# A layer's products in pairs of 64 rows: 24 products of M2's first column group, in two PSUM banks

## The chip, the cores and the metric

The kernel runs on one core of one Trainium2 chip. The metric is the device time of one execution in microseconds (us). The median of three runs of the kernel before is 946.14 us (946.11 to 946.61).

## The reference

Attention with a sigmoid in place of the softmax feeds two layers of the same form (from a 768-wide token to 2048 and back). Only the last layer is touched by the change.

```python
scores = scale * np.matmul(q, k.transpose(0, 1, 3, 2)) - np.log(S)
attn = 1.0 / (1.0 + np.exp(-scores))
x = np.matmul(attn, v)            # 4 x 12 heads, 448 x 64, then tokens x 768
...
h = x @ w_in                      # layer 1: 1792 x 768 by 768 x 2048
g = s * np.maximum(h, 0.0) ** 2 + b
x = g @ w_out                     # 1792 x 2048 by 2048 x 768
...
h = x @ w_in                      # layer 2, the last one
g = np.maximum(h, 0.0) + alpha * np.minimum(h, 0.0)
out = g @ w_out
```

## The kernel before, in words

**Work.** After the attention stage each layer is done for two token groups of 2 x 512 and 2 x 384 tokens, one after the other, and for each group an "in" phase (`in_phase`, or `first_phase` for the very first) and an "out" phase (`out_phase`) follow. Each matrix product is taken by a seven-product scheme on 2 x 2 blocks (Strassen-Winograd): products M1 to M7 of sums and differences of the blocks, put together by additions. `out_phase` goes through them in the order M1, M2, M5, M6, M7, M4, M3 (`OUT_ORDER`, line 41), and for each through three column groups, k = 0, 1, 2, so it has 21 groups of products.

**A group of products.** The operands are full-precision numbers, each split into a rounded part ("hi", by a cast on ScalarE, line 519) and the rest ("lo", a subtraction on VectorE, line 522). For one piece of 128 rows of the contraction TensorE then does three products: hi weights by lo data, hi by hi, lo by hi. A group of `out_phase` has eight such pieces, 24 products of 128 rows, 128 output partitions and 512 or 384 columns, all added up in one PSUM bank. `mm_group` (lines 605 to 622) writes them; it is called once for each of three chunks of pieces (3, 3 and 2, `CHUNKS`).

```python
nc.tensor.matmul(d, wh_, ml_, start=first and k == 0, stop=False, **opt)
nc.tensor.matmul(d, wh_, mh_, start=False, stop=False, **opt)
nc.tensor.matmul(d, wl_, mh_, start=False, stop=last and k == n, **opt)
```

**Names.** `ring` holds the split weights of one group (three places, in turn, filled from `raw`, which SP's queue loads). `gb` holds the split data of a product, in three chunks: in the 512-column group gb_117 to gb_119 for M1 and gb_120 to gb_122 for M2. `g` holds the data before they are split; the differences that later products need are taken in place (line 532), and the layer's nonlinearity ends in a scale-and-add on VectorE (line 690). `tmp` holds what has been read out of PSUM.

**Banks.** There are eight. In `out_phase` M1's three column groups go to banks 0 to 2, those of M2 to banks 6, 7 and 6 (`6 + k % 2`), M5's to 3 to 5. When M2's group k has ended, VectorE adds the bank to `tmp` (`padd`, line 639), and the sum is stored.

**Order.** The program lists every operation with its engine, a duration and what it reads and writes (`Plan.add`). TensorE's order is the order of the list. For the other engines a planner (`Plan.order`, `Plan.place`) takes at each step the operation that can start first by its own estimates and, among those, the one that is needed soonest; a small random shift, drawn for each operation in the order of the list, is added to that due time. Each engine works through its order in sequence, and waits where an operand isn't ready or a buffer isn't free.

Of the kernel before, what the change touches and what calls it, by code (L numbers as in the profile page):

```python
# [17 lines left out]
P = 128  # L18
# [29 lines left out]
T = (512, 384)  # L48
# [25 lines left out]
class Plan:  # L74
# [9 lines left out]
    def add(self, eng, dur, fn, r=(), w=(), lat=0.06):  # L84
        i = len(self.ops)
        self.uses.append([sorted({c[1] for c in x if c[0] == "t"}) for x in (r, w)])
        r, w = ([c for c in x if c[0] != "t"] for x in (r, w))
        deps = set()
        for c in r:
            if c in self.writer:  # L90
                deps.add(self.writer[c])
        for c in w:
            if c in self.writer:
                deps.add(self.writer[c])
            deps.update(self.readers.get(c, ()))
        for c in r:
            self.readers.setdefault(c, set()).add(i)
        for c in w:
            self.writer[c] = i
            self.readers[c] = set()  # L100
        deps.discard(i)
        self.ops.append((eng, dur, lat, deps, fn))
# [149 lines left out]
def cells(r, n):  # L252
    a = r.base + r.off
    return [("t", r.of)] + [("s", c) for c in range(a // CELL, -(-(a + n) // CELL))]


def sb(r, n):
    return r.ap[:, r.off : r.off + n]
# [3 lines left out]
def tile_kernel(  # L262
# [11 lines left out]
    nc = tc.nc  # L274
# [3 lines left out]
    D = vt.shape[5]  # L278
# [21 lines left out]
    add = plan.add  # L300
# [64 lines left out]
    def dve_t(n, psum=False):  # L365
        return 0.075 + 1.037e-3 * n
# [8 lines left out]
    PE_LAT = 0.25  # L375
    MM = (0.2269, 0.1745)

    def tmp():
        return TMP.pop(0)

    def free(x):
        TMP.append(x)
# [102 lines left out]
    def unit(m, kind, i):  # L485
        at, n = i * UNIT, UNIT
        dst = entry(range(8 * i, 8 * i + 8))
        raw = RAW[n_unit[1] % NRAW]
        n_unit[1] += 1
        load(  # L490
            sb(raw, n), w32[m, kind][:, at : at + n], n,
            [("d", m, kind, 8 * i + j) for j in range(8)], cells(raw, n),
        )
        split(dst, dst + n, raw, n)
# [21 lines left out]
    def split(hi, lo, src, n, rows=1, step=None):  # L516
        (h, ch), (l, cl), (x, cx) = (part(r, n, rows, step) for r in (hi, lo, src))
        n *= rows
        add("ACT", act_t(n), lambda: nc.scalar.copy(h, x), cx, ch)  # L519
        add(  # L520
            "DVE", dve_t(n),
            lambda: nc.vector.tensor_tensor(  # L522
                out=l, in0=x, in1=h.bitcast(F32), op=ALU.subtract
            ),
            cx + ch, cl,
        )

    def minus(o, x, y, n, rows=1, step=None):
        (o_, co), (x_, cx), (y_, cy) = (part(r, n, rows, step) for r in (o, x, y))
        add(  # L530
            "DVE", dve_t(rows * n),
            lambda: nc.vector.tensor_tensor(out=o_, in0=x_, in1=y_, op=ALU.subtract),  # L532
            cx + cy, co,
        )
# [20 lines left out]
    def g_place(par, p, j=0):  # L555
        return G[par] + (8 * p + j) * T[par]
# [45 lines left out]
    def bank(k, n=S, c=0):  # L602
        return ps[:, k, c : c + n]

    def mm_group(par, dst_bank, terms, first, last, more=False):

        t = T[par]
        r = [("p", dst_bank)] if not first else []
        for wh, wl, mh, ml in terms:
            r += cells(wh, P) + cells(wl, P) + cells(mh, t) + cells(ml, t)  # L610

        def f():
            n = len(terms) - 1
            for k, (wh, wl, mh, ml) in enumerate(terms):
                wh_, wl_, mh_, ml_ = sb(wh, P), sb(wl, P), sb(mh, t), sb(ml, t)
                d = bank(dst_bank, t)
                opt = {"skip_group_check": more}
                nc.tensor.matmul(d, wh_, ml_, start=first and k == 0, stop=False, **opt)  # L618
                nc.tensor.matmul(d, wh_, mh_, start=False, stop=False, **opt)  # L619
                nc.tensor.matmul(d, wl_, mh_, start=False, stop=last and k == n, **opt)  # L620

        add("PE", 3 * MM[par] * len(terms), f, r, [("p", dst_bank)], PE_LAT)

    def pcopy(dst, k, n, func=None):
        d = sb(dst, n)

        def f():
            if func is None:
                nc.scalar.copy(d, bank(k, n))
            else:  # L630
                nc.scalar.activation(d, bank(k, n), func)

        add("ACT", act_t(n, True), f, [("p", k)], cells(dst, n))

    def padd(dst, k, other, n, c=0):
        d, o = sb(dst, n), sb(other, n)
        add(
            "DVE", dve_t(n, True),
            lambda: nc.vector.tensor_tensor(out=d, in0=bank(k, n, c), in1=o, op=ALU.add),  # L639
            [("p", k)] + cells(other, n), cells(dst, n),  # L640
        )
# [157 lines left out]
    def store(dst, src, n, w):  # L799
        d, x = dst, sb(src, n)  # L800
        add("SP", dma_t(n), lambda: nc.sync.dma_start(out=d, in_=x), cells(src, n), w, DMA_LAT)

    def put(m, g, p, k, src):

        row, nb = divmod(p, 2)
        dc = 2 * k + row
        t = T[g]
        if m == 0:
            kh, i = divmod(dc, KH)
            o = (2 * kh + nb) * XB[g] + i * t  # L810
            store(x_dram[1, g][:, o : o + t], src, t, [("x", 1, g, 2 * kh + nb, i)])
        else:
            c = 2 * g * T[0] + nb * t
            store(out[dc * P : (dc + 1) * P, c : c + t], src, t, [])

    def out_phase(m, g, par, middle):
        t, r = {}, {}
        P1, P2, P3, P4 = range(4)
        make = {
            "M1": (P1, None), "M5": (P1, (P2, P1)), "M2": (P3, None), "M6": (P1, (P4, P1)),  # L820
            "M7": (P2, (P4, P2)), "M4": (P1, (P3, P1)), "M3": (P4, None),
        }

        def prepare(i):
            src, diff = make[OUT_ORDER[i]]
            for (j0, j1), o in zip(CHUNKS, GB[par][i % 2]):
                n = (j1 - j0) * T[par]
                if diff:
                    minus(g_place(par, src, j0), g_place(par, diff[0], j0), g_place(par, diff[1], j0), n)
                split(o, o + n, g_place(par, src, j0), n)  # L830

        prepare(0)
        for i, x in enumerate(OUT_ORDER):
            if i + 1 < 7:
                prepare(i + 1)
            if i in middle:
                middle[i]()
            for k in range(NDP):
                unit(m, "out", i * NDP + k)
                bk = {"M2": 6 + k % 2, "M5": 3 + k, "M3": 3 + k}.get(x, k)  # L840
                more = x in ("M6", "M7", "M4", "M3")
                for (j0, j1), o in zip(CHUNKS, GB[par][i % 2]):
                    terms = [
                        (*ring[(i * NDP + k) * 8 + j], o + (j - j0) * T[par], o + (j1 - j0 + j - j0) * T[par])
                        for j in range(j0, j1)
                    ]
                    mm_group(par, bk, terms, not more and j0 == 0, j1 == 8, more)
                if x == "M1":
                    t[k] = tmp()
                    pcopy(t[k], bk, T[par])  # L850
                elif x == "M2":
                    padd(t[k], bk, t[k], T[par])
                    put(m, g, 0, k, t[k])
                    free(t[k])
                elif x == "M6":
                    r[k] = tmp()
                    pcopy(r[k], bk, T[par])
                elif x == "M7":
                    y = tmp()
                    pcopy(y, bk, T[par])  # L860
                    padd(y, 3 + k, y, T[par])
                    put(m, g, 3, k, y)
                    free(y)
                elif x == "M3":
                    padd(r[k], bk, r[k], T[par])
                    put(m, g, 1, k, r[k])
                    free(r[k])
                elif x == "M4":
                    y = tmp()
                    pcopy(y, bk, T[par])  # L870
                    put(m, g, 2, k, y)
                    free(y)
# [131 lines left out]
    for _ in range(NWARM):  # L1004
        for h in range(2):
            for j in range(2):
                rows = slice(j * D, (j + 1) * D)
# [3 lines left out]
                    start=True, stop=True,  # L1011
# [47 lines left out]
    for n, (m, g) in enumerate(phases):  # L1059
        par = n % 2  # L1060
# [79 lines left out]
```

## Time and profile before

| | |
|---|---|
| median of three runs | 946.14 us |
| the profiled execution | 946.52 us |
| its span, first to last instruction | 944.5 us |
| busy: TensorE products, VectorE, ScalarE | 938.5, 732.1, 650.7 us |
| the layers' products by 512 and by 384 columns, mean spacing in an undisturbed group | 0.227 and 0.173 us |
| M2 for k=0 in the last layer, 512-column group: start, start of the next group | 666.55, 671.99 us |
| the same, 384-column group | 865.07, 870.23 us |

A product's own duration in the trace (0.39 us at 512 columns) is longer than the spacing, since products are pipelined; what counts is from start to start. The same holds for VectorE: an operation of 1.75 us is followed by the next after 1.67 us.

### The profile page before, as it was taken

How to read it: one execution, taken by the hardware profiler on the slowest of the kernel's cores; microseconds unless marked ns; L12 is line 12 of the kernel's file. 1: busy time of each engine (PE TensorE's matmuls, PEld its weight loads, DVE VectorE, ACT ScalarE, POOL GpSimd, SP SyncE). 2: the span in 40 equal slices, each digit the busy share in tenths (PEclk: the TensorE clock that was granted, in tenths of full speed). 3: DMA queues.
4: the chain of work that ended last, by engine and by line, in shares of the span. 5: the costliest groups of instructions: out<-in, count | busy, mean ns of one | idle time of the engine just before them, and what ended most of it. 6: DMA issues, size and time to landing. Idle time of an engine off the chain costs nothing.

```text
span 944.5 us, 13900 instructions
## 1 busy us (share of the span) xinstructions
PE 938.5 (99%) x5424; PEld 778.5 (82%) x5424; DVE 732.1 (78%) x882; ACT 650.7 (69%) x796; POOL 0.2 (0%) x4
## 2 busy tenths in 40 slices
PE   9999999999999999999999999999999999999998
PEld 4333358888888889999999988888888899999998
DVE  1748668987999996677999959788985936689962
ACT  6989977868955754888967546667745536677551
POOL 0000000000000000000000000000000000000000
PEclk9999999999999999999999999999999999999999
DMA  8998999994647989898657787645334443443542
GB/s 303 324 317 304 335 312 316 322 303 158 239 145 243 316 297 339 306 311 271 227 165 238 229 291 236 234 132 193 120 113 122 149 141 112 134 135 120 151 136 96
DMA packets 81248, 210.88 MB, mean 223 GB/s; under 512 B 7712, under 2 KB 42912, under 8 KB 81184
## 3 DMA queue, kind: packets, MB, share of 16 engines
q1 hardware_dynamic: 81184, 210.01, 67.7%
q8 instruction: 42, 0.69, 0.3%
q14 instruction: 22, 0.18, 0.0%
HBM read 152.58 MB, written 57.41 MB: 222 GB/s over the span
## 4 chain that ended last, share of the span: by engine, by line
PE 88%; ACT 5%; DVE 5%; issue 2%; DMA 1%; DVEq 0%; ACTq 0%
PE ps L618 25%; PE ps L620 25%; PE ps L619 25%; PE ps L934 7%; PE ps L972 7%; DVE gb L522 1%; DVE ring L522 1%; ACT ring L519 1%; ACT g L706 1%; DVE g L639 1%; DMA raw<-w0in 1%; ACT neg L685 0%; ACT g L703 0%; ACT g L667 0%; ACT gb L519 0%
## 5 line engine op out<-in xcount | busy, mean ns | idle before, releaser
L618 PE MATMUL ps<-gb,ring 128*128 128x512 f32 (+1 forms) x672 | 243.4, 362 | 1.6 <-DVE gb L522 1.6
L619 PE MATMUL ps<-gb,ring 128*128 128x512 f32 (+1 forms) x672 | 243.0, 362 | 0.0
L620 PE MATMUL ps<-gb,ring 128*128 128x512 f32 (+1 forms) x672 | 243.0, 362 | 0.0
L519 ACT CAST ring<-raw 128x1024 fp32r<-128x1024 f32 x147 | 154.3, 1050 | 115.6 <-PE ps L619 102.3
L522 DVE TENSOR_TENSOR ring<-raw,ring 128x1024 fp32r<-128x1024 f32 x147 | 179.2, 1219 | 63.2 <-ACT ring L519 63.2
L620 PE MATMUL ps<-xo,ring 128*128 128x384 f32 (+1 forms) x504 | 177.6, 352 | 0.0
L619 PE MATMUL ps<-xo,ring 128*128 128x384 f32 (+1 forms) x504 | 177.6, 352 | 0.0
L618 PE MATMUL ps<-xo,ring 128*128 128x384 f32 (+1 forms) x504 | 177.6, 352 | 0.0
L618 PEld LDWEIGHTS ps<-gb,ring 128*128 128x128 f32 x672 | 126.1, 188 | 16.0 <-DVE gb L522 3.0
L620 PEld LDWEIGHTS ps<-gb,ring 128*128 128x128 f32 x672 | 126.1, 188 | 13.2
L619 PEld LDWEIGHTS ps<-gb,ring 128*128 128x128 f32 x672 | 126.1, 188 | 13.0
L522 DVE TENSOR_TENSOR gb<-g,gb 128x1536 fp32r<-128x1536 f32 (+3 forms) x84 | 116.3, 1395 | 13.1 <-ACT gb L519 7.1
L519 ACT CAST gb<-g 128x1536 fp32r<-128x1536 f32 (+3 forms) x84 | 99.3, 1196 | 23.0 <-PE ps L620 15.2
L619 PEld LDWEIGHTS ps<-xo,ring 128*128 128x128 f32 x504 | 94.6, 188 | 6.7
L620 PEld LDWEIGHTS ps<-xo,ring 128*128 128x128 f32 x504 | 94.6, 188 | 6.6
L618 PEld LDWEIGHTS ps<-xo,ring 128*128 128x128 f32 x504 | 94.6, 188 | 6.5
L950 ACT ACTIVATE sg<-ps,bias 128x896 f32<-128x896 f32 x84 | 83.4, 1013 | 13.5 <-PE ps L934 12.8
L639 DVE TENSOR_TENSOR g<-ps,g 128x512 f32<-128x512 f32 (+1 forms) x104 | 64.1, 623 | 23.8 <-PE ps L620 17.9
L934 PE MATMUL ps<-kq 64*64 64x448 f32 x672 | 78.5, 545 | 0.0
L972 PE MATMUL ps<-sg,v 64*64 64x448 f32 x672 | 77.1, 536 | 0.0
L532 DVE TENSOR_TENSOR g<-g 128x1536 f32<-128x1536 f32 (+3 forms) x48 | 66.0, 1391 | 0.0
L618 PE MATMUL ps<-xo,rinq 128*128 128x512 f32 x168 | 65.5, 390 | 0.0
(63 smaller groups left out, 993.8 us busy)
## 6 DMA issues: line engine op xcount, KB each, us to landing
r<-in_w_in SPq DMA_DIRECT2D x28, 768.0 KB, 6.3
raw<-w0out SPq DMA_DIRECT2D x42, 512.0 KB, 4.0
raw<-w1in SPq DMA_DIRECT2D x42, 512.0 KB, 3.6
raw<-w1out SPq DMA_DIRECT2D x42, 512.0 KB, 3.5
r<-in_w_out SPq DMA_DIRECT2D x18, 768.0 KB, 6.1
raw<-w0in SPq DMA_DIRECT2D x21, 512.0 KB, 5.4
kq<-in_qk SPq DMA_DIRECT2D x23, 448.0 KB, 4.8
w1out<-quada SPq DMA_DIRECT2D x6, 1344.0 KB, 7.5
```

What stands on the lines that cost most here:

```text
L519: add("ACT", act_t(n), lambda: nc.scalar.copy(h, x), cx, ch)
L522: lambda: nc.vector.tensor_tensor(out=l, in0=x, in1=h.bitcast(F32), op=ALU.subtract),
L532: lambda: nc.vector.tensor_tensor(out=o_, in0=x_, in1=y_, op=ALU.subtract),
L618: nc.tensor.matmul(d, wh_, ml_, start=first and k == 0, stop=False, **opt)
L619: nc.tensor.matmul(d, wh_, mh_, start=False, stop=False, **opt)
L620: nc.tensor.matmul(d, wl_, mh_, start=False, stop=last and k == n, **opt)
L639: lambda: nc.vector.tensor_tensor(out=d, in0=bank(k, n, c), in1=o, op=ALU.add),
L706: lambda: nc.scalar.activation(h, h, AF.Identity, bias=b_t, scale=s_t),
L934: nc.tensor.matmul(ps[h * D : (h + 1) * D, k + j, :S], a.ap[rows, S + k0 : S + k0 + D], a.ap[rows, :S], start=True, stop=True,)
L950: lambda: nc.scalar.activation(o, i, AF.Sigmoid, bias=sb(BIAS, 1), scale=QKSCALE),
L972: nc.tensor.matmul(ps[j * D : (j + 1) * D, k + h, :S], va[keys, v : v + D], a.ap[keys, j * S : (j + 1) * S], start=first, stop=last,)
```

## The change

In `out_phase` of the last layer, for M2 and k=0, every 128-row product becomes two 64-row products: rows 0 to 63 into bank 6 as before, rows 64 to 127 into bank 7. VectorE then adds both banks to `tmp`, one after the other. This is done once in each token group; nothing else in the code changes.

```diff
+                if other is not None:
+
+                    for i, (w, x) in enumerate(((wh_, ml_), (wh_, mh_), (wl_, mh_))):
+                        for b, rows in ((dst_bank, slice(0, D)), (other, slice(D, P))):
+                            nc.tensor.matmul(
+                                bank(b, t), w[rows], x[rows], start=first and k == 0 and i == 0,
+                                stop=last and k == n and i == 2, **opt,
+                            )
+                    continue
...
-        add("PE", 3 * MM[par] * len(terms), f, r, [("p", dst_bank)], PE_LAT)
+        w = [("p", k) for k in (dst_bank, other) if k is not None]
+        add("PE", 3 * MM[par] * len(terms), f, r + w[1:] if not first else r, w, PE_LAT)
...
-                    mm_group(par, bk, terms, not more and j0 == 0, j1 == 8, more)
+                    other = 7 if m == 1 and x == "M2" and k == 0 else None
+                    mm_group(par, bk, terms, not more and j0 == 0, j1 == 8, more, other)
...
                 elif x == "M2":
                     padd(t[k], bk, t[k], T[par])
+                    if other is not None:
+                        padd(t[k], other, t[k], T[par])
```

The planner keeps its old duration for the group. Since the list has one more operation in each of the two phases, the random shifts of all operations behind it are other ones, and the order moves a little around and after these places.

VectorE, 512-column group, around the addition of M2's group k=0 (tmp_90; ring_60 to ring_62 are the ring's places). Before:

```order
L522 TENSOR_TENSOR gb_117<-g_115,gb_117 128x1536
L522 TENSOR_TENSOR gb_122<-g_115,gb_122 128x1024
L532 TENSOR_TENSOR g_115<-g_115 128x1536
L522 TENSOR_TENSOR ring_62<-raw_68,ring_62 128x1024
L690 SCALAR_TENSOR_TENSOR g_115<-neg,nal,g_115 128x512
L522 TENSOR_TENSOR gb_118<-g_115,gb_118 128x1536
L639 TENSOR_TENSOR tmp_90<-ps,tmp_90 128x512
L690 SCALAR_TENSOR_TENSOR g_115<-neg,nal,g_115 128x512
```

The same place in the changed kernel:

```order
L522 TENSOR_TENSOR gb_122<-g_115,gb_122 128x1024
L522 TENSOR_TENSOR gb_117<-g_115,gb_117 128x1536
L532 TENSOR_TENSOR g_115<-g_115 128x1536
L522 TENSOR_TENSOR ring_62<-raw_68,ring_62 128x1024
L700 SCALAR_TENSOR_TENSOR g_115<-neg,nal,g_115 128x512
L522 TENSOR_TENSOR gb_118<-g_115,gb_118 128x1536
L700 SCALAR_TENSOR_TENSOR g_115<-neg,nal,g_115 128x512
L649 TENSOR_TENSOR tmp_90<-ps,tmp_90 128x512
L532 TENSOR_TENSOR g_115<-g_115 128x1024
L649 TENSOR_TENSOR tmp_90<-ps,tmp_90 128x512
L522 TENSOR_TENSOR ring_60<-raw_67,ring_60 128x1024
```

The split of gb_122 stands ahead of that of gb_117 now, one more scale-and-add stands ahead of the addition, and between the additions of the two banks there is a difference of 1024 columns.

TensorE, the end of M2's group k=0 and the start of group k=1 (on ring_61) in the changed kernel, with the engines that a product waits for:

```order
L622 MATMUL ps<-gb_122,ring_60 128x512 [waits DVE_49]
L622 MATMUL ps<-gb_122,ring_60 128x512
L622 MATMUL ps<-gb_122,ring_60 128x512 [waits Activation_49]
L622 MATMUL ps<-gb_122,ring_60 128x512 x9
L627 MATMUL ps<-gb_120,ring_61 128x512 [waits DVE_49]
```

Before, the last of these, the first product of k=1, had no wait; the products of the group k=0 were one row each and no pairs.

VectorE, 384-column group, from the addition of M2's group k=0 (tmp_86) on, in the changed kernel:

```order
L649 TENSOR_TENSOR tmp_86<-ps,tmp_86 128x384
L700 SCALAR_TENSOR_TENSOR g_116<-neg,nal,g_116 128x384
L649 TENSOR_TENSOR tmp_86<-ps,tmp_86 128x384
L522 TENSOR_TENSOR ring_60<-raw_67,ring_60 128x1024
L532 TENSOR_TENSOR g_116<-g_116 128x768
```

The third row is new; what stands before the first and the other rows are as before.

## Rows read from the trace of the kernel before

**Rows 1.** The page, part 1: TensorE's busy time.

```profile
PE 938.5 (99%) x5424; PEld 778.5 (82%) x5424; DVE 732.1 (78%) x882; ACT 650.7 (69%) x796; POOL 0.2 (0%) x4
```

**Rows 2.** Waits of TensorE, whole span, then from 672 us: total, times, longest.

```profile
PE ps L618 <- DVE gb L522: 1.6, 4, 0.7
...
PE ps L618 <- DVE gb L522: 1.2, 2, 0.7
```

**Rows 3.** Timeline of TensorE, 512-column group: start us, us, operation.

```profile
666.55 0.39 PE L618 MATMUL ps<-gb,ring 128*128 128x512 f32 x1
...
671.76 0.39 PE L620 MATMUL ps<-gb,ring 128*128 128x512 f32 x1
671.99 0.39 PE L618 MATMUL ps<-gb,ring 128*128 128x512 f32 x1
```

**Rows 4.** Timeline of TensorE, 384-column group.

```profile
865.07 0.33 PE L618 MATMUL ps<-gb,ring 128*128 128x384 f32 x1
...
869.08 0.44 PE L618 MATMUL ps<-gb,ring 128*128 128x384 f32 x1 [0.72 <-DVE gb L522]
869.36 0.34 PE L619 MATMUL ps<-gb,ring 128*128 128x384 f32 x1
...
870.06 0.33 PE L620 MATMUL ps<-gb,ring 128*128 128x384 f32 x1
870.23 0.33 PE L618 MATMUL ps<-gb,ring 128*128 128x384 f32 x1
```

**Rows 5.** Timeline of VectorE, 512-column group; [idle before <- what ended it].

```profile
664.87 2.89 DVE L522 TENSOR_TENSOR gb<-g,gb 128x1536 fp32r<-128x1536 f32 x2 [0.81 <-ACT gb L519]
667.68 1.75 DVE L532 TENSOR_TENSOR g<-g 128x1536 f32<-128x1536 f32 x1
669.35 1.22 DVE L522 TENSOR_TENSOR ring<-raw,ring 128x1024 fp32r<-128x1024 f32 x1
670.48 0.74 DVE L690 SCALAR_TENSOR_TENSOR g<-neg,nal,g 128x512 f32<-128x512 f32 x1
671.14 1.75 DVE L522 TENSOR_TENSOR gb<-g,gb 128x1536 fp32r<-128x1536 f32 x1
672.81 0.68 DVE L639 TENSOR_TENSOR tmp<-ps,tmp 128x512 f32<-128x512 f32 x1
673.41 0.74 DVE L690 SCALAR_TENSOR_TENSOR g<-neg,nal,g 128x512 f32<-128x512 f32 x1
```

**Rows 6.** Timeline of VectorE, 384-column group.

```profile
868.08 0.95 DVE L522 TENSOR_TENSOR gb<-g,gb 128x768 fp32r<-128x768 f32 x1
...
870.74 0.55 DVE L639 TENSOR_TENSOR tmp<-ps,tmp 128x384 f32<-128x384 f32 x1
871.21 0.61 DVE L690 SCALAR_TENSOR_TENSOR g<-neg,nal,g 128x384 f32<-128x384 f32 x1
871.74 1.21 DVE L522 TENSOR_TENSOR ring<-raw,ring 128x1024 fp32r<-128x1024 f32 x1
```

**Rows 7.** Chain that ended last, attention stage: start us, us, operation, records.

```profile
3.88 3.73 PE ps L934 x24
...
8.36 0.75 PE ps L934 x8
```

**Rows 8.** Timeline of TensorE, from the attention's last products to the first layer's.

```profile
129.21 2.42 PE L972 MATMUL ps<-sg,v 64*64 64x448 f32 x24
131.56 0.50 PE L618 MATMUL ps<-xo,rinq 128*128 128x512 f32 x1
```

**Rows 9.** DMA issues: KB each, median us to landing.

```profile
raw<-w1out SPq DMA_DIRECT2D x42, 512.0 KB, 3.5
```

**Rows 10.** Stretches: length, then busy PE, PEld, DVE, ACT, POOL, PEclk, DMA.

```profile
3.88:7.60 3.72, 3.72 (x28) 1.33 (x32) 0.00 (x0) 1.68 (x2) 0.00 (x0) 1.00 0.88 291
...
941.20:942.20 1.00, 0.00 (x0) 0.00 (x0) 0.51 (x1) 0.00 (x0) 0.00 (x0) 1.00 0.00 0
942.20:944.50 2.30, 0.00 (x0) 0.00 (x0) 0.00 (x0) 0.00 (x0) 0.00 (x0) 1.00 0.23 86
```

More of the change, by code (lines that the diff above doesn't have):

```diff
@@ L603, in bank, with mm_group @@
         return ps[:, k, c : c + n]
-    def mm_group(par, dst_bank, terms, first, last, more=False):
+    def mm_group(par, dst_bank, terms, first, last, more=False, other=None):
         t = T[par]
```

## The prediction

> **What bounds the kernel now.** I read the page's busy times first: TensorE is busy 938.5 us of a span of 944.5 us [rows 1], so the end moves only by what its stream gains or loses. The table of waits comes next: TensorE waits for splits on VectorE four times, 1.6 us in all, the longest 0.7 us [rows 2]. So a product slot saved is time saved, and a new wait of this engine is time lost, nearly one for one. After 672 us two waits are left, 1.2 us together [rows 2]; that is the most that a later stage could give back.
>
> Then the two places that the change touches. In the 512-column token group, M2 for k=0 starts at 666.55 us, its last product at 671.76 us, and the next group, M2 for k=1, at 671.99 us, with no gap [rows 3]: 5.44 us for 24 products, 0.227 us each. In the 384-column group it is 865.07 us to 870.23 us, with one wait inside, before the product at 869.08 us [rows 4]; the next group again follows without a gap. Last I read VectorE there. It adds the first bank at 672.81 us and 870.74 us [rows 5, 6], after the group has ended, and before the change nobody on TensorE waits for that.
>
> **Part 1: the products.** 24 products over 128 rows become 24 pairs over 64. No row shows a 64x128 pair; the nearest are the attention products, tiles of 64 rows by 64 columns in sets of four, of which two share the output partitions and go to two banks, as the new pairs do. Eight records (two sets) take 0.75 us [rows 7], so a set of 448 columns takes 0.375 us in two passes, 0.188 us a pass with four tiles side by side. Scaled by columns that is 0.188 x 512/448 = 0.215 us for a pair and 24 x 0.215 = 5.15 us for the group: 0.29 us less than 5.44. The other end is two halves one after the other: 48 x 0.227 = 10.9 us. I take the first, since the attention row is the same arrangement with more tiles. In the 384-column group the last six products wait for a split that VectorE ends at 868.08 + 0.95 = 869.03 us [rows 4, 6], so only six pairs can gain, under 0.1 us.
>
> TensorE changes from 128-row to 64-row tiles and back. The one change of that kind in the trace stands after the attention: the last 24 records (six sets of 0.375 us) start at 129.21 us, so the first full product was due at 131.46 us; it starts at 131.56 us [rows 8]. So 0.1 us each way at most, about what the pairs save in the first group. Neither counts if the next wait is longer, and it is.
>
> **Part 2: the wait.** This decides. Bank 7 now holds half of M2 for k=0, and M2 for k=1 writes into bank 7 next. Its first product must wait until VectorE has read the bank; before, that product had no wait (order on TensorE). Behind it stands the whole in-order stream of TensorE. VectorE also works in order, so the wait ends when it reaches the second addition.
>
> 512-column group. In the new order VectorE has, from the split of gb_117 on: split 1536, difference 1536, ring split, scale-and-add, split 1536, scale-and-add, addition of bank 6, difference 1024, addition of bank 7. The split of gb_117 started at 664.87 us, having waited 0.81 us for its cast [rows 5]. That cast sits behind the first pieces of M1's last group, which the change doesn't touch; the split of gb_122 now fills the wait ahead of it. So I start at 664.87 us and take the spacings of starts [rows 5]: 1536-column pass 669.35 - 667.68 = 1.67, ring or 1024-column pass 1.13, scale-and-add 0.66, addition 0.60. Sum 1.67 + 1.67 + 1.13 + 0.66 + 1.67 + 0.66 = 7.46, so bank 6 is added at 672.33 us; the group's last product ends by 671.76 + 0.39 = 672.15 us at the latest, so VectorE does not wait. Then 0.60 + 1.13 brings bank 7 to 674.06 us, and its 0.68 us to 674.74 us. From VectorE's end to TensorE's start it took 869.08 - 869.03 = 0.05 us [rows 4, 6]. So k=1 starts at 674.79 us instead of 671.99: **2.80 us**. Floor: additions back to back behind the last product, 672.15 + 0.60 + 0.68 + 0.05 = 673.48 us, 1.5 us. Ceiling: no idle time filled, and one scale-and-add (0.66) more ahead of 672.81 us: 673.47 + 0.60 + 1.13 + 0.68 + 0.05 = 675.93 us, 3.9 us.
>
> 384-column group. The order up to the addition of bank 6 is the old one, at 870.74 us [rows 6]; then a scale-and-add, then bank 7. So 870.74 + 0.47 + 0.53 = 871.74 us, + 0.55 + 0.05 = 872.34 us instead of 870.23: **2.11 us**. Floor, without the scale-and-add: 1.6 us; ceiling, with another scale-and-add slipping ahead: 2.6 us.
>
> Restart: after the wait at 869.08 us the second product came 0.28 us later instead of 0.173 [rows 4]; 0.1 us twice, **0.2 us**.
>
> **Costed at nothing.** The two additions themselves (0.60 and 0.47 us) lie behind the wait that is already counted; VectorE then is 0.6 us later but TensorE 2.8 us later, so it has more room than before for the splits of the next groups. The first store now waits for the second addition, and a load stands behind it on SP's queue; it is for M5's third group, which comes four groups of 5.44 us after k=1 starts, and a load lands in 3.5 us [rows 9]. In the 384-column group two loads move behind the stores of k=1 and k=2; they serve M6, three groups of 4.16 us after the later of these stores.
>
> **Sum**: 2.80 + 2.11 + 0.2 = 5.11 us. The profiled execution took 946.52 us, so it would take 951.6 us; the median of the three runs is 946.14 us, 0.38 us less, and I forecast against it: **951.3 us**, 0.54% slower. The floors give 949.4 us and the ceilings 952.8 us.
>
> **Rivals.**
> A. The pairs do not run side by side. For it: no row shows two tiles with 128 columns. Against it: the attention sets. If they run one after the other, the first group ends 5.44 us later, and VectorE's slack of 0.18 us (672.33 - 672.15) doesn't cover that: 5.3 us more. In the second, 48 products of 0.173 us from 865.07 us start the last one at 873.2 us, end it at 873.5 us, and 0.47 + 0.53 + 0.55 + 0.05 brings 875.1 us: 2.8 us more. Together 959.4 us. The Trainium skill ("TensorE: Matmul & The Clock Gate", Part 3, measured speedup) gives four row tiles only 3.07 times one. An estimate by that figure: a pair is 4/3.07 = 1.3 slots, the first group 7.1 us, and the time some 1.5 us above my forecast. The attention rows, where four tiles fit in 0.188 us a pass, speak against it; but those tiles are not row tiles alone.
>
> B. TensorE's clock falls in the wait. The wait of 3 us is four times the longest in the rows. At the start, with TensorE just out of idleness, 24 records took 3.73 us where 2.25 (three times 0.75) is usual [rows 7]: 1.5 us lost, although the granted clock reads 1.00, the higher of its two levels, there too [rows 10]. One fall gives 952.8 us, two 954.3 us. Against it: after the last product TensorE is idle from 941.2 us to the end at 944.5 us, and the granted clock still reads 1.00 [rows 10].
>
> C. Not slower: VectorE is ready in time. If it adds bank 7 so early that both waits together stay under 1.9 us, the result is no change, and if there is no wait at all, the pairs' 0.29 + 0.1 us give 945.8 us. For it: VectorE idles 0.81 us close before [rows 5]. Against: a floor of 1.5 + 1.6 us, as both additions can start only after the group's last product. It decides at a start of k=1 before 672.9 us and 871.2 us.
>
> **How the numbers follow.** A measurement of this kernel can tell about 0.2%, 1.9 us, from no change. My forecast, with the sizes between floors and ceilings: 0.78. A: 0.09. B: 0.10. C: 0.03. The range of 949.8 to 954.0 us reaches from near the floors (less part of the 1.2 us of later waits) through the ceilings to one fall of the clock and to pairs that overlap in part; it leaves out A's far end, C and two falls. Faster 0.01, same 0.03, slower 0.96.
>
> **What would show it.** In the table of waits, a new line of TensorE waiting for the addition into tmp on VectorE, twice, some 3 and 2 us. M2 k=0 in about 5.2 us, pairs starting 0.215 us apart; M2 k=1 starting near 674.8 and 872.3 us (the latter plus the first delay, 875.2 us). All groups after it at the old 5.44 and 4.16 us. Pairs 0.45 us apart would show A; products 0.45 us apart after the wait would show B; no wait and no shift would make the prediction wrong.

## The result, and the profile after

The changed kernel takes **954.79 us** (median of three runs, 954.52 to 955.07) against 946.14 us: a ratio of 1.009 (95% interval 1.0067 to 1.0113), slower as forecast, but by 8.65 us where 5.1 were forecast, and 0.8 us above the end of the range. The profiled execution took 954.79 us, with a span of 952.9 us against 944.5 us.

The waits of TensorE in the changed kernel (total, times, longest):

```profile
PE ps L627 <- DVE tmp L649: 4.6, 2, 2.7
...
PE ps L627 <- DVE gb L522: 0.6, 2, 0.5
PE ps L622 <- DVE gb L522: 0.5, 1, 0.5
```

The first line is new, and it is the one that the prediction named: TensorE waits twice for the addition into tmp. The waits for splits, 1.6 us before [rows 2], are 1.1 us now.

TensorE's timeline in the 512-column group, to be held beside [rows 3]:

```profile
666.10 0.39 PE L629 MATMUL ps<-gb,ring 128*128 128x512 f32 x1
666.42 5.76 PE L622 MATMUL ps<-gb,ring 64*128 64x512 f32 x48
674.85 0.50 PE L627 MATMUL ps<-gb,ring 128*128 128x512 f32 x1 [2.67 <-DVE tmp L649]
675.18 0.40 PE L628 MATMUL ps<-gb,ring 128*128 128x512 f32 x1
...
675.88 0.51 PE L628 MATMUL ps<-gb,ring 128*128 128x512 f32 x1
676.19 0.63 PE L629 MATMUL ps<-gb,ring 128*128 128x512 f32 x1
676.61 0.63 PE L627 MATMUL ps<-gb,ring 128*128 128x512 f32 x1
...
678.75 0.63 PE L629 MATMUL ps<-gb,ring 128*128 128x512 f32 x1
679.17 0.51 PE L627 MATMUL ps<-gb,ring 128*128 128x512 f32 x1
679.52 0.39 PE L628 MATMUL ps<-gb,ring 128*128 128x512 f32 x1
679.75 0.39 PE L629 MATMUL ps<-gb,ring 128*128 128x512 f32 x1
```

M2's second group starts at 674.85 us (forecast 674.79). Then comes what the sum did not hold: after five products at the usual pace, products start 0.43 us apart, at half pace, until 679.5 us. The stretches of the same time, and of the same thing in the 384-column group (columns as in [rows 10]; PEclk is the third number from the end), say why:

```profile
674.80:676.00 1.20, 1.15 (x5) 0.98 (x6) 1.20 (x2) 0.47 (x1) 0.00 (x0) 1.00 0.33 121
676.00:679.40 3.40, 3.40 (x10) 2.61 (x9) 3.40 (x3) 0.00 (x0) 0.00 (x0) 0.50 0.60 193
679.40:700.00 20.60, 20.60 (x92) 17.06 (x92) 16.11 (x14) 8.04 (x7) 0.00 (x0) 1.00 0.33 100
...
877.40:880.80 3.40, 3.40 (x12) 3.40 (x12) 3.40 (x4) 0.83 (x1) 0.00 (x0) 0.50 0.63 198
880.80:949.00 68.20, 68.20 (x394) 68.20 (x394) 39.86 (x39) 29.93 (x35) 0.00 (x0) 1.00 0.41 123
```

In two stretches the granted clock is 0.50, the lower of the two levels (1.2 instead of 2.4 GHz). Neither is a stretch of waiting: TensorE is busy throughout, and each begins after the products have come back, 1.2 us and 0.5 us after. The wait ahead of the second one, in the 384-column group, stands behind the shorter wait for a split that was there before [rows 4]:

```profile
873.68 1.32 PE L622 MATMUL ps<-gb,ring 64*128 64x384 f32 x12 [0.52 <-DVE gb L522]
876.94 0.44 PE L627 MATMUL ps<-gb,ring 128*128 128x384 f32 x1 [1.94 <-DVE tmp L649]
```

VectorE in the 512-column group, beside [rows 5]:

```profile
663.59 2.95 DVE L522 TENSOR_TENSOR gb<-g,gb 128x1024 fp32r<-128x1024 f32 x2
666.57 1.76 DVE L532 TENSOR_TENSOR g<-g 128x1536 f32<-128x1536 f32 x1
668.25 1.22 DVE L522 TENSOR_TENSOR ring<-raw,ring 128x1024 fp32r<-128x1024 f32 x1
669.38 0.74 DVE L700 SCALAR_TENSOR_TENSOR g<-neg,nal,g 128x512 f32<-128x512 f32 x1
670.04 1.75 DVE L522 TENSOR_TENSOR gb<-g,gb 128x1536 fp32r<-128x1536 f32 x1
671.71 0.74 DVE L700 SCALAR_TENSOR_TENSOR g<-neg,nal,g 128x512 f32<-128x512 f32 x1
672.38 0.68 DVE L649 TENSOR_TENSOR tmp<-ps,tmp 128x512 f32<-128x512 f32 x1
672.98 1.21 DVE L532 TENSOR_TENSOR g<-g 128x1024 f32<-128x1024 f32 x1
674.11 0.68 DVE L649 TENSOR_TENSOR tmp<-ps,tmp 128x512 f32<-128x512 f32 x1
```

The two additions start at 672.38 and 674.11 us; the prediction had worked out 672.33 and 674.06 us.

Where the time went, by groups of TensorE's products (from the first product of a group to the first of the next, us):

| group | before | after | more |
|---|---|---|---|
| 512 columns: M1 k=2, its end (change to 64-row tiles) | 5.44 | 5.53 | 0.09 |
| M2 k=0 with the wait behind it | 5.44 | 8.42 | 2.98 |
| M2 k=1 (start after the wait, slow stretch) | 5.44 | 7.17 | 1.73 |
| 384 columns: M1 k=2, its end | 4.16 | 4.25 | 0.09 |
| M2 k=0 with the wait behind it | 5.16 | 7.17 | 2.01 |
| M2 k=1 | 4.16 | 5.87 | 1.71 |
| sum | | | 8.61 |

All other groups of these phases are as before, and the sum is the difference of the spans (8.4 us) but for 0.2 us that this execution had gained earlier. So 5.2 us belong to waits and tile changes, and some 3.4 us to the two groups behind the waits (starts after a wait and slow stretches).

### The profile page after: what moved, and what is told of

Read it like the earlier page. It is cut to its first block, busy times and chain, and to the rows that moved or that the text cites. A ratio compares the mean times of both kernels' runs of the same rounds, so it can differ in the third digit from the quotient of the medians.

```text
span 952.9 us, 13996 instructions
## 1 busy us (share of the span) xinstructions
PE 942.8 (99%) x5472; PEld 781.2 (82%) x5472; DVE 734.3 (77%) x884; ACT 650.5 (68%) x796; POOL 0.2 (0%) x4
## 4 chain that ended last, share of the span: by engine, by line
PE 91%; DVE 5%; ACT 2%; issue 2%; DVEq 0%
PE ps L627 26%; PE ps L628 26%; PE ps L629 26%; PE ps L947 7%; PE ps L985 7%; DVE gb L522 2%; DVE ring L522 1%; DVE g L700 1%; DVE g L532 1%; ACT ring L519 1%; ACT neg L695 0%; DVE g L649 0%; ACT gb L519 0%; ACT g L697 0%; DVE tmp L649 0%
## 5 line engine op out<-in xcount | busy, mean ns | idle before, releaser
L627 PE MATMUL ps<-gb,ring 128*128 128x512 f32 (+1 forms) x656 | 239.0, 364 | 5.2 <-DVE tmp L649 4.6
L629 PE MATMUL ps<-gb,ring 128*128 128x512 f32 (+1 forms) x656 | 238.7, 364 | 0.0
L628 PE MATMUL ps<-gb,ring 128*128 128x512 f32 (+1 forms) x656 | 238.4, 363 | 0.0
L627 PEld LDWEIGHTS ps<-gb,ring 128*128 128x128 f32 x656 | 124.1, 189 | 19.9 <-DVE tmp L649 5.3
L628 PEld LDWEIGHTS ps<-gb,ring 128*128 128x128 f32 x656 | 124.1, 189 | 12.8
L629 PEld LDWEIGHTS ps<-gb,ring 128*128 128x128 f32 x656 | 123.9, 189 | 12.9
```

## The experiments

Theory 1: the waits for bank 7 cost what was worked out, and they also bring the two stretches at the lower clock. Its rivals: the 64-row pairs let the clock fall by themselves (theory 2), or the pairs are slow (theory 3). On the chip of the first four runs the kernel before took 946.81 us, on that of the next three 946.78 us; the ratio is to that. The times expected of the first four runs were worked out from 946.14 us, so some 0.7 us of a miss there is the chip.

| run | us | ratio (95% interval) | stretches at 0.50 ahead of the last product |
|---|---|---|---|
| changed kernel | 954.79 | 1.009 (1.0067 to 1.0113) | 2 |
| pairs, second half in bank 5 | 947.86 | 1.0008 (0.9998 to 1.0017) | 0 |
| no pairs, two banks | 956.09 | 1.0096 (1.0081 to 1.0111) | 2 |
| bank 7 added first | 949.71 | 1.0024 (1.0014 to 1.0033) | 0 |
| wait filled, twelve products | 952.65 | 1.0061 (1.0046 to 1.0076) | 0 |
| wait filled, four products | 951.99 | 1.0053 (1.0038 to 1.0068) | 0 |
| pairs in two groups, bank 5 | 947.72 | 1.0009 (1.0000 to 1.0018) | 0 |
| 384-column group alone | 950.56 | 1.0035 (1.0021 to 1.0049) | 1 |

### The pairs without the wait

```diff
-                    other = 7 if m == 1 and x == "M2" and k == 0 else None
+                    other = 5 if m == 1 and x == "M2" and k == 0 else None
```

> The second half of the pairs goes to bank 5, which no product writes until M5's third group, four groups later; the pairs stay. Theory 1 (the loss is the wait for bank 7, 2.9 + 2.1 us, and two stretches at the granted clock of 0.50 that these waits bring on, 1.7 us each): both waits and both stretches are gone, and what is left is the pairs' own cost, from the changed kernel's rows some 0.1 us for each switch of tile shape and 0.007 us for each 384-column pair: 946.3 to 947.0 us. Theory 2 (the pairs of half-height tiles let the clock fall, the wait only costs itself): both stretches at 0.50 stay, 949.5 to 950.5 us. Theory 3 (the pairs themselves are slow): over 948 us with the clock at 1.00.

Measured: a ratio of 1.0008, and no stretch at the lower clock among the products. TensorE at the same place of this run:

```profile
667.74 0.39 PE L629 MATMUL ps<-gb,ring 128*128 128x512 f32 x1
668.05 5.76 PE L622 MATMUL ps<-gb,ring 64*128 64x512 f32 x48
673.74 0.50 PE L627 MATMUL ps<-gb,ring 128*128 128x512 f32 x1
674.08 0.40 PE L628 MATMUL ps<-gb,ring 128*128 128x512 f32 x1
```

The same 48 products are there, and the next group follows at once. Theory 2 is out: the pairs alone do not move the clock. So is theory 3. What they cost can be read at both ends: from the last 128-row product to the first pair 0.31 us and from there to the second pair 0.33 us instead of 0.227, and the same again on the way back (0.32 and 0.34). That is 0.2 us a change, 0.4 us a token group, 0.8 us in all: the size of the loss that is left, though the interval of the ratio holds no loss as well. The Trainium skill ("TensorEngine Tiling (Array Packing)", Key Properties) says that a change of the tiling mode drains the engine. The rows show a start that comes 0.09 us late at each change, which fits; a full drain they do not show, since by the profile's durations the last product (0.39 us) still runs when the first pair starts.

### The wait without the pairs

Every third product goes to bank 7, whole.

```diff
-                        for b, rows in ((dst_bank, slice(0, D)), (other, slice(D, P))):
-                            nc.tensor.matmul(
-                                bank(b, t), w[rows], x[rows], start=first and k == 0 and i == 0,
-                                stop=last and k == n and i == 2, **opt,
-                            )
+                        b = other if i == 2 else dst_bank
+                        nc.tensor.matmul(
+                            bank(b, t), w, x, start=first and k == 0 and i in (0, 2),
+                            stop=last and k == n and i in (1, 2), **opt,
+                        )
```

> No pairs: products of 128 rows as in the kernel before, 24 a group, but every third one (lo weights) goes to bank 7 and the other two to bank 6, so that two banks are to be added and M2's second group waits for bank 7 as in the changed kernel. Theory 1: the waits (3.0 and 2.2 us) and both stretches at 0.50 come back without any pair, 953.8 to 954.8 us. Theory 2: the waits alone, the clock stays at 1.00, 950.8 to 951.6 us.

Measured: 1.0096, as much as the change, and in us 1.3 above the range given. The stretches of this run:

```profile
674.40:681.20 6.80, 6.00 (x14) 4.74 (x15) 6.80 (x7) 1.05 (x1) 0.00 (x0) 0.50 0.37 116
681.20:700.00 18.80, 18.80 (x84) 15.53 (x84) 14.07 (x12) 7.10 (x7) 0.00 (x0) 1.00 0.31 78
879.20:882.60 3.40, 3.40 (x13) 3.40 (x12) 3.40 (x5) 0.83 (x1) 0.00 (x0) 0.50 0.68 210
```

The wait without a single 64-row product brings the slow stretches, the first of them here twice as long, from within the wait on (M2's second group takes 8.39 us, against 7.17 in the changed kernel). That is 1.2 us more; with the chip's 0.7 us it covers the miss. So a second bank that the next group needs is enough for a loss of this size; of the changed kernel's, only the 0.2 us of tile changes in the table are the pairs'.

### A shorter wait

```diff
-                    padd(t[k], bk, t[k], T[par])
                     if other is not None:
                         padd(t[k], other, t[k], T[par])
+                    padd(t[k], bk, t[k], T[par])
```

> The pairs and bank 7 stay; VectorE adds bank 7 first and bank 6 second. The wait for bank 7 ends one addition and one operation earlier: M2's second group starts some 1.1 us later than in the kernel before in each token group, instead of 2.9 and 2.1. Theory 1: with waits of little over 1 us the clock stays at 1.00, 948.2 to 949.0 us. Theory 2: the stretches at 0.50 stay, 951.6 to 952.4 us. If one of the two waits still brings the clock down, some 950.2 us, and the length from which it does lies between.

Measured: 1.0024, 2.3 us (by the medians 2.9), and the clock stays up. TensorE at the same place, and its waits:

```profile
672.36 0.50 PE L627 MATMUL ps<-gb,ring 128*128 128x512 f32 x1 [0.94 <-DVE tmp L649]
672.69 0.39 PE L628 MATMUL ps<-gb,ring 128*128 128x512 f32 x1
672.92 0.39 PE L629 MATMUL ps<-gb,ring 128*128 128x512 f32 x1
```

```profile
PE ps L627 <- DVE tmp L649: 1.9, 2, 1.0
```

Swapping two lines takes away 2.7 us of waiting (4.6 to 1.9) and, with it, both slow stretches. The loss comes down to between a quarter and a third.

### The wait filled

Twelve more products follow the last pair, of operands that are there already, into bank 4, which nobody reads before it is overwritten; their results are not used.

```diff
+                    if last and k == n:
+                        for _ in range(12):
+                            nc.tensor.matmul(bank(4, t), wh_, mh_, start=True, stop=True)
                     continue
```

> The changed kernel with twelve more products of 128 rows (the group's last hi by hi product again, into bank 4, which nobody reads before M5 overwrites it) behind the pairs in each token group, where TensorE waits for bank 7: 12 x 0.227 = 2.7 us and 12 x 0.173 = 2.1 us, so the wait is filled and hardly longer. Theory 1: M2's second group starts when it did, the clock stays at 1.00, and the 3.3 us of the two slow stretches are gone: 951.0 to 951.8 us. Theory 2: the clock falls as before, 954.5 to 955.2 us.

TensorE in this run:

```profile
668.06 5.76 PE L622 MATMUL ps<-gb,ring 64*128 64x512 f32 x48
673.75 3.05 PE L628 MATMUL ps<-gb,ring 128*128 128x512 f32 x12
676.63 0.40 PE L630 MATMUL ps<-gb,ring 128*128 128x512 f32 x1
676.86 0.39 PE L631 MATMUL ps<-gb,ring 128*128 128x512 f32 x1
```

The stretch from there to behind the last product (the 1.00 is the clock):

```profile
668.00:950.00 282.00, 279.08 (x1513) 259.83 (x1512) 196.10 (x197) 154.61 (x202) 0.00 (x0) 1.00 0.42 125
```

M2's second group starts 8.57 us after the first (8.42 in the changed kernel), so the time lost to bank 7 is the same and a little more. But behind it the products run at full pace: that group takes 5.45 us instead of 7.17, in the 384-column group 4.16 instead of 5.87. The granted clock is 1.00 throughout. The ratio is 1.0061, in us some 5.8 instead of 8.6; the run is 0.9 us above what was expected by the median (952.65), 0.7 us of which is the other chip's base. Useless work saves 1.7 us in each group behind a wait, for 0.2 us that it adds to the wait itself: the slow stretches come from TensorE's idleness and not from what it waits for.

### How long a wait

The same with four products (`range(4)`).

> The changed kernel with four more products behind the pairs in each token group instead of twelve: M2's second group starts where it did, but of TensorE's wait 4 x 0.227 = 0.9 us and 4 x 0.173 = 0.7 us are filled, so that from start to start some 2.1 us stay empty in the 512-column group and 1.6 us in the 384-column group. It tells from which wait on the clock falls, between the 1.3 us that left it at 1.00 and the 2.3 us that did not. If a wait of 2.1 us still brings a stretch at 0.50 and one of 1.6 us doesn't: the changed kernel's ratio less 1.7 us, 952.5 to 953.6 us on a chip where the kernel before takes 946.1 to 946.8. If both do: 954.2 to 955.6 us. If neither does: 951.0 to 952.7 us. A theory in which only the wait counts, whatever TensorE does in it, expects 954.5 us or more.

```profile
672.52 1.20 PE L628 MATMUL ps<-gb,ring 128*128 128x512 f32 x4
675.24 0.50 PE L630 MATMUL ps<-gb,ring 128*128 128x512 f32 x1 [1.52 <-DVE tmp L652]
675.58 0.40 PE L631 MATMUL ps<-gb,ring 128*128 128x512 f32 x1
```

Both waits, and the clock of the stretch to behind the last product:

```profile
PE ps L630 <- DVE tmp L652: 2.6, 2, 1.5
```

```profile
666.00:949.00 283.00, 277.21 (x1500) 257.26 (x1499) 196.89 (x197) 155.36 (x202) 0.00 (x0) 1.00 0.42 125
```

Neither wait brings the clock down: waits of 1.5 and 1.1 us, by the profile's idle time, left it at 1.00, those of 2.7 and 1.9 us in the changed kernel did not. M2's second group takes 5.60 us here, so of the 7.17 us in the changed kernel 1.57 us are the slow stretch and 0.16 us are the start after a wait; in the 384-column group (4.27 us) it is 1.60 and 0.11 us. The median is within the range given for this case, and the ratio, 1.0053, is that of the twelve products (1.0061) within the intervals.

### The pairs' own cost, doubled

```diff
-                    other = 5 if m == 1 and x == "M2" and k == 0 else None
+                    other = 5 if m == 1 and x == "M2" and k in (0, 2) else None
```

> The pairs' own cost, doubled: second half in bank 5 (no wait), pairs for M2's groups k=0 and k=2, so four changes of tile shape and back. From the rows of the run with bank 5 each change there and each change back costs 0.19 us and a pair exactly what a single product costs. If that is the pairs' whole price, the two groups of pairs in each token group cost 4 x 0.4 = 1.6 us against the kernel before, twice the 0.8 us of the run with bank 5: a ratio of 1.0014 to 1.0020. If the 0.8 us was noise of the chip or moved order, the ratio stays within 1.0010.

Measured: 1.0009 (1.0000 to 1.0018), hardly more than with one group of pairs. The interval holds both theories, and the median is against a full doubling, so the times are inconclusive. The trace has the tile changes four times in each token group, at about the price expected (0.5 us for a group of pairs where 0.4 was): in the 512-column group, the groups from M1's third to M5's first take 5.53, 5.69, 5.69, 5.69 and 5.60 us against 5.44 us, 1.0 us more in all, where the run with one group of pairs has 5.53, 5.69 and 5.60 us, 0.5 us more.

### One token group alone

```diff
-                    other = 7 if m == 1 and x == "M2" and k == 0 else None
+                    other = 7 if (m, g) == (1, 1) and x == "M2" and k == 0 else None
```

> The change in the 384-column token group alone; the 512-column group is as in the kernel before. If the two groups' losses are separate, the loss is this group's wait (2.1 us), its slow stretch (1.7 us) and the change of tiles ahead of it (inside the wait for the most part): 3.6 to 4.4 us more than the kernel before. If the second stretch at 0.50 came only because of the first one, it is gone: 1.9 to 2.6 us more.

Measured: 1.0035, 3.3 us, by the median 3.8 us. The waits and stretches of this run:

```profile
PE ps L627 <- DVE tmp L649: 1.9, 1, 1.9
```

```profile
873.23 0.44 PE L627 MATMUL ps<-gb,ring 128*128 128x384 f32 x1 [1.93 <-DVE tmp L649]
```

```profile
874.70:878.10 3.40, 3.40 (x13) 3.40 (x12) 3.40 (x5) 0.84 (x1) 0.00 (x0) 0.50 0.54 159
```

One wait, one slow stretch, which here begins 1.5 us after the products have come back: the second stretch does not need the first, and the losses add up (3.8 us here, 4.8 us in the table's 512-column rows, 8.6 us together).

How many slow stretches come is not the same in every run. By the mean granted clock, four of this kernel's five runs have room for one stretch of 3.4 us (0.998) and one for two (0.996, 950.68 us); of the changed kernel's three runs two have 0.996 and the third, 954.52 us, 0.998. The times of these runs do not stand apart from the others, and their traces are not kept, so what makes up for a stretch more or less stays open. With waits of 1.5 us and less no run shows room for one.

### Why the pairs gain nothing

The prediction took 0.215 us for a pair from the attention's rows. The changed kernel's 48 records (entries of the trace, here one for each 64-row product) take 5.76 us; less 0.39 us, the last pair's own duration, and 0.1 us for the late second pair, 5.27 us are 23 spacings of 0.229 us: a single product's 0.227, or hardly more. Attention's operands are plain f32, those of the layers are in the rounded format. Two further kernels, measured once each, tell the format from the tile's width: with bank 5, the pairs' operands are read as f32, in tiles of 64 x 128 and of 64 x 64.

```diff
-                                bank(b, t), w[rows], x[rows], start=first and k == 0 and i == 0,
+                                bank(b, t), w[rows].bitcast(F32), x[rows].bitcast(F32), start=first and k == 0 and i == 0,
```

> Why the pairs gained nothing: the kernel with bank 5, with the pairs' operands read as full 32-bit numbers (f32, as in the attention products) in place of the rounded format, still 64 rows by 128 columns. One product is then two records per tile. The attention sets took 0.3755 us for a record of 448 columns, 2 x 448 cycles at 2.4 GHz (0.3733) plus 0.002 us; the pairs in the rounded format took 0.2267 us for 512, 0.2133 plus 0.013 us. If the number format makes the difference, a record of 512 columns comes every 0.429 us (0.4267 + 0.002). If the 128 columns of the weights do, every 0.440 us (0.4267 + 0.013). The run is some 30 us longer, since a product costs four times as much.

> The same with tiles of 64 rows by 64 columns, four for each product, in f32: the attention's tiles in this place. Both theories expect a record of 512 columns every 0.429 us; another spacing here would say that neither format nor columns make the difference but something else in this stage (the longer rows, the accumulation over many products).

TensorE, 64 x 128, the whole group and then twelve of its records:

```profile
667.05 20.87 PE L622 MATMUL ps<-gb,ring 64*128 64x512 f32 x96
...
668.88 2.74 PE L622 MATMUL ps<-gb,ring 64*128 64x512 f32 x12
```

And 64 x 64:

```profile
666.77 20.83 PE L623 MATMUL ps<-gb,ring 64*64 64x512 f32 x192
```

Between 6 and 48 pairs of records lie 20.87 - 2.74 = 18.13 us for 42, less 0.1 us for the first: 0.429 us a record, two passes of 512 columns (0.4267 us at 2.4 GHz) plus 0.002 us. The quarter tiles take the same time. So neither the height nor the width of the tile is what costs; the format is: a product in the rounded format takes 0.013 us more than its columns, in full tiles and in pairs alike, and a record in f32 0.002 us more. Both kernels took longer, as they must (973.88 and 973.49 us; the kernel before 947.24 us on that chip). What in the rounded format costs those 0.013 us stays open; a product in it is also only half as long as an f32 record.

## Why the prediction had the wait right and the clock wrong

- **The bound** (TensorE, nearly one for one): right. The table of groups adds up to the span.
- **The wait (part 2)**: right. It had 2.80 and 2.11 us; from the start of M1's third group on, M2's second group comes 3.07 and 2.10 us later than before (2.98 + 0.09 and 2.01 + 0.09), and 0.2 us of the first is the lead that this execution had. The chain on VectorE (672.33, 674.06 us) came out 0.05 us later. The runs with bank 5 and with bank 7 first show that this wait is the cause.
- **The start after a wait**: 0.1 us each; measured 0.16 and 0.11 us (the run with four products).
- **The step that failed: rival B**, the clock. It was given a chance of 0.10 and kept out of the sum, and it happened twice: "two 954.3 us" was the right line (954.79 measured). The two slow stretches cost 3.17 us; the terms of the sum came to 5.44 us (5.17 for waits and tile changes, 0.27 for the starts) where 5.11 were forecast. What was wrong was the argument against it: TensorE is idle at the program's end for 3.3 us with a clock of 1.00 [rows 10], so an idle time of 3 us was taken to be safe. The change shows 0.50 behind idle times of 2.7 and 1.9 us, and only after products had come back. The reading of the end was the luck of one execution besides: in the traces of the changed kernel and of the run with bank 5 the clock does fall there, 3.0 and 2.4 us after the last product has ended (at 949.53 and 942.92 us). First the changed kernel's row, then that of bank 5:

```profile
952.50:952.90 0.40, 0.00 (x0) 0.00 (x0) 0.00 (x0) 0.00 (x0) 0.00 (x0) 0.50 0.00 0
...
945.40:946.40 1.00, 0.00 (x0) 0.00 (x0) 0.00 (x0) 0.00 (x0) 0.00 (x0) 0.50 0.00 0
```

The rows of the start [rows 7], 24 records at less than their usual pace, were the better guide, and the 1.00 beside them [rows 10] was no evidence against it: in the trace of the kernel before, the record of the clock begins only at 6.56 us, and there the pace of the sets goes from one in 0.75 us (up to 6.05 us) to one in 0.38 (from 6.69 us on). The price of a fall read from them, 1.5 us, was near the measured 1.57 and 1.60 us in part by luck: in the run with bank 7 first the same 24 records take 2.78 us instead of 3.73, a loss of 0.5 us. And the range (to 954.0 us) allowed for one fall, though both waits are of the same kind and would bring two.
- **The pairs (part 1)**: side by side, as forecast; rival A is out. Their size was wrong: no gain of 0.29 us, since the attention rows have another number format. It cost the forecast nothing, because the wait hides the group's end. An estimate by the Trainium skill's figure ("TensorE: Matmul & The Clock Gate", Part 3, measured speedup; 3.07 for four row tiles) was 1.3 products for a pair. Here a pair takes 0.229 us and a product 0.227, so that figure, of four tiles of 32 rows, does not carry over to two of 64.
- **Costed at nothing**: right. No group after M2's second is longer than before, and no new wait for a load appears.
- **Rival C** (VectorE in time): out, as its floor said.

## What to carry to other kernels

Before a group of products is given a second bank, look at who writes that bank next: here it was the very next group, and its wait, not the products, made nearly the whole loss; a bank that is free for four groups brought it down to about the tile changes (0.8 us). When a stall on TensorE is priced, add what comes behind it: here waits of 1.9 us and more cost 1.6 us on top in four of the five traced cases and 2.8 us once, in a stretch at half clock that lay, but for that one, behind the return of the products. Where no other bank is free, shortening the wait did more (two lines swapped, 8.6 to 2.3 us) than filling it (5.0 and 5.8 us). A price that is scaled from other rows should come from rows of the same number format.

## What the runs showed of the hardware that was not expected

- The granted clock went to 0.50 for 3.4 us behind waits of 1.9 and 2.7 us (once, behind a wait of 2.9 us in the run without pairs, for 6.8 us), beginning up to 1.5 us after TensorE was busy again; behind waits of 1.5 us and less it stayed at 1.00.
- A pair of 64-row tiles in two banks costs what one 128-row product costs (0.229 and 0.227 us), and a change of tile height 0.2 us each way.
- An f32 record of two passes comes every 0.429 us at 512 columns, 0.002 us over its cycles; a product in the rounded format every 0.227 us, 0.013 us over them, in 128-row tiles and, but for 0.002 us, in 64-row pairs.
